# An attention and mixture-of-experts kernel on one core: instruction order taken from a list, and the last batch's attention weights turned by TensorE

## The chip, the cores and the metric

The kernel runs on one core of a Trainium2 chip. Its time is the device time of a run in microseconds (us); three runs of the kernel before gave 221.73, 222.76 and 223.56 us, with a median of 222.76. The engines are called by the profile's names: PE is TensorE (PEld its weight loads), DVE is VectorE, ACT is ScalarE, POOL is GpSimd, SP is SyncE, which here issues nearly all DMAs.

## The reference

Two steps follow each other. The first is an attention with 32 "inducing" rows, once in each direction, over four batches of 11456 tokens with 128 channels:

```python
def mab(q, kv):
    s = scale * (q @ kv.transpose(0, 2, 1))
    s = s - s.max(-1, keepdims=True)
    a = np.exp(s)
    a /= a.sum(-1, keepdims=True) + 1e-09
    return a @ kv
h = mab(I, x)                 # 32 rows per batch
attn = mab(x, h)              # every token: 32 weights times h
```

The second is a layer of 8 experts on the tokens whose skip score is positive: each such token takes the expert with the highest gate logit and adds the expert's output times its gate probability.

```python
do_compute = x @ w_skip > 0
e_idx = np.argmax(xc @ w_gate, axis=1)
y[mask] = gate_w[mask, None] * (np.maximum(xc[mask] @ w1[e], 0.0) @ w2[e])
out[do_compute] = xc + y
```

All data are float32.

## The kernel before

A batch is cut into six groups of 2048 tokens (the last has 1216; in batch 0 the small one comes first). A group is cut into four quarters q, so that a tile of a group's 32 weights per token has 4 x 32 = 128 partitions and 512 columns.

**First pass** over a group (`first`): PE forms the scores (L387), DVE their maxima (L393), ACT the exponentials (L397). PE turns them (L431) and turns x itself (L447), both into PSUM banks that ACT or DVE copy out (`copy`, L340 on ACT, L342 on DVE), and sums into the 32 rows h (L457). Five groups have their x turned by DVE from a second load instead (L424). **Between the passes** (`middle`) the rows h are normed (L540, L557), the batch's expert is chosen (L576, L577, then the DVE steps L590 to L595 and a register load on SP), its weights w1 and w2 are loaded (L719, L721; PE uses w1 at L644), and y, the expert's output for each of the 32 rows, comes out (L697, L708).

**Second pass** (`second`, `emit`): PE forms scores of 32 rows by 512 columns in each quarter (L748). DVE turns them in blocks of 32 by 32 into tile e, which has the tokens on its partitions (L753), and takes the maxima (L755); POOL or DVE subtract them (L759); ACT takes the exponentials (L762); POOL folds the halves (L768), DVE sums (L772), POOL or DVE norm (L778). DVE then turns e back into u1 (`back`, L783), with a weight's row on the partition. From u1 PE takes the gate logits. Batches 0 to 2 do it for full groups in the form called "quarters" (L840, with L844, L851, L864 behind it, and L873 to bring the gates to their place); the last batch and the small groups have 16 matmuls of 32 by 256 (L792), turned back by DVE (L801), with L803, L806, L810, L822 behind them. The weights times the gate are tile v (L882), which DVE turns into u2 (L783 again). `emit` sums hr times u1 and yr times u2 for the group into four banks (L935), copies these into two tiles `o` (L340, L342) and stores each (L945).

Tiles come from rings of fixed size: ten x tiles, eight PSUM banks, four `o`, five e and u1, two u2.

**What sets the order.** Every step is an `Op` with what it needs and the buffers it takes. `best_order` reads a rank for every step from the table PLACES, and `in_order` runs a small planner over them, with one estimated cost per step and engine. Its result is the order in which the steps are written, for each engine and for SP's DMA queue alike; where a step could run on two engines, it chose the engine. On the chip each engine works through its own list in that order and waits on semaphores.

Of the kernel before, what the change touches and what calls it, by code (L numbers as in the profile page):

```python
# [64 lines left out]
def in_order(ops, bufs):  # L65


    LAT, SLACK, RATE, LAND = 0.12, 0.1, 380.0, 1.8
    users, left = {}, {}
    for o in ops:  # L70
        left[o] = len(o.need) + len(o.behind)
        for n in o.need + o.behind:
            users.setdefault(n, []).append(o)
        for b in (*o.take, *o.free):
            b.end = b.idx = None
    free = dict.fromkeys((e for o in ops for e in o.cost), 0.0)
    wire = 0.0
    taken = {t: [] for t in bufs}
    bank = [None] * BANKS
    done = []  # L80

    def entry(o):

        at = [(e, max((d.end + (LAT if d.eng != e else 0.0) for d in o.need), default=0.0), c,
               o.spare if e == "DVE" else 0.0) for e, c in o.cost.items()]
        return o, at, sum(b.tag == "ps" for b in o.take), [b.tag for b in o.take if b.tag != "ps"]

    ready = [entry(o) for o in ops if not left[o]]
    while ready:
        up = sorted((0.0 if v is None else v.end + LAT, i) for i, v in enumerate(bank) if v is None or v.end is not None)  # L90
        c, first = [], {}
        for r in ready:
            o, at, n, tags = r
            t0 = 0.0
            if n:
                if len(up) < n:
                    continue
                t0 = up[n - 1][0]
            for tag in tags:
                k = len(taken[tag]) - bufs[tag]  # L100
                if k >= 0:
                    v = taken[tag][k].end
                    if v is None:
                        break
                    t0 = max(t0, v + LAT)
            else:
                _, t, e = min((max(t0, a, free[e]) + w + s, max(t0, a, free[e]), e) for e, a, w, s in at)
                c.append((t, e, r))
                if t < first.get(e, 1e9):
                    first[e] = t  # L110
        assert c, "a cycle of buffers"
        low = min(first.values())
        t, eng, r = min((v for v in c if v[0] <= low + SLACK and first[v[1]] == low), key=lambda v: (v[2][0].rank, v[0]))
        ready.remove(r)
        o = r[0]
        o.eng = eng
        free[eng] = o.end = t + o.cost[eng]
        if o.size:
            wire = max(wire, t) + o.size / RATE
            o.end = wire + LAND  # L120

        got = [i for v, i in up if v <= max(t, up[r[2] - 1][0])][-r[2]:] if r[2] else []
        for b in o.take:
            if b.tag == "ps":
                b.idx = got.pop()
                bank[b.idx] = b
            else:
                b.idx = len(taken[b.tag]) % bufs[b.tag]
                taken[b.tag].append(b)
        for b in o.free:  # L130
            b.end = o.end
        done.append((t, o))
        for u in users.get(o, []):
            left[u] -= 1
            if not left[u]:
                ready.append(entry(u))
    return [o for _, o in sorted(done, key=lambda v: v[0])], max(o.end for o in ops)


def best_order(ops, bufs):  # L140


    assert len(PLACES) == 3 * len(ops)
    for i, o in enumerate(ops):
        r, d, e = (DIGITS.index(c) for c in PLACES[3 * i:3 * i + 3])
        o.rank, o.spare = 64 * r + d, SPARES[e]
    return in_order(ops, bufs)[0]


DIGITS = "0123456789ABCDEFGHIJKLMNOPQRSTUVWXYZabcdefghijklmnopqrstuvwxyz-_"  # L150
SPARES = (0.0, 0.4, 1.0, 3.0, -0.5)
PLACES = (
    "Ez0Ad0DG09c0B70EU4FS0Bx3BB0HB4BM0Aq2CR09B0B50As02R08l07F07U3B209e3BJ07714n07t03b0AM12k05T02502n02A02w01H03z00u00w11U01F1"
    "1-01s42t02634602Z01f04S08O03n09C04k00v04h01_01m25u08R44W0Aj26y02I07S09l0Bg06v04R08E25-05_05P07c14D01Z17H02l33305Q00B00E0"
    "0001Q00i00420500Z10b00840r00231S00140C01C00m01A01D05y04Z05z02_04c02p41r03f41i03405v24B05B05F02Y06L03u04420I01a01z01g00S0"
    "2e00n00X23x02031p05M05727M03742x02o37X03-07o0Be0AX0Ae04z08Q03g04v02r06b03L26o01j34y02T07403W06Z47I02901q0Bf44s09A02L03F0"
    "4E06M02-02V03p4BY41h03804F26F23e07N31v2430B905809n13H08544G06938L04t03N04C09j08X03r0A008M3AD04Y0680Ci3BT17307v07a2BV07b0"
    "8A0Bp2990D117z04727e04A09805x08203Y01O09r04235k34I02O02K17x05i08F27D27p0AI0A209017A09m17g08z06P0Ao04m0500A602G04b0550Di4"
    "9h45l05d09x3Ba2Ap06j29P2AG0Av06D08i3F906V38U0A834O05X0Ai06p0D20A708N03M04K1DP09T0A10Ee1Ak3BQ0DR3Du3CM08g0Ge09G0Eq0AR09Z2"
    "6l0BU0Bu02q09Y02f03907V03o05S03E06h07m02206f44u02d23A04L01b04802703q04w01E21w02z04_09v15W07K06606Q43U05H09_04907n01o04e0"  # L160
    "8P06U09d16J0310C203P02a07f06H04N07O06d06S04V08D06141N02g3CO0DU13209303m02m03J06C09206q07y0A_27E06n12s06z07i0Bd25s05K18_0"
    "6305E07Z07Y09i09k05j18Z0DK28-0D426E03_43i0BC03y01y02W00x00L02c00g00W01X11I00a10700302434H01k00f02b00s07B00G30V01801207w0"
    "4q01T00O01P20P00c45N04p03Q44j0Ca46G02X27009S09106W09q06O0BN04r04047P1F209D0Dr43t35O01538t22v0BI06a0Gd1Ac0B_14a08h26t0670"
    "3B07l09J07Q04f05R06_1A927r03C06u37614i0DY12U3Bz0FP0G20E227-07k47W09y3710DQ09M0Ag0Da0Dp0De0830972El3BF05t0ET28r48w0Cd3AV3"
    "Cb0C80Ay0G53DF0G42FG0AT39K0Gl07h0An0Cg0BE0GF0Db0C51722B10Fb0951GM16-0D013S2Bt0GX0G60AY2DX0CS2CL0Fe39O0D_09H0880CW0GZ0BP0"
    "7C04-48926X05n09I28j3Dq08635A1D50840H80Fy3EO0DB1Gz0Fg0EJ05m0G70Gi0Fa0H20HL0Ef0Fn4Gk0Af0FZ1A51Eh0Eb2GK3Do0Cw0CQ0Bn04l0ED0"
    "E80Bv0EY0A303v0By06007_03O0Bh49t0Gm04g08p2Dt06B0Fu0Ev37d0Dj05108b0410B-05r06k03G04x08104U0EH09U06T05Y0DO0Gw0Fl08T0D709g0"
    "A-08d2AE0FI3Bl0Cz48q0E42FQ0Br0FJ0EA0D90E709b0B30EI0CY1FV0Bk09-0A409w0Aa04J08W0E505404X09V0EW05D1ER08k26R03s4EQ04Q2Ah06Y0"
    "Fw0C90Ax0CE0C30Ga48a0Cx1BX0At3CZ0Dg38o0En03D00j00l00K00o01Y00T03K00k23w02P20h01e00D10900e00A00z00601L02C00N01002j06K00-0"
    "1V01J02H25J00y4B40E_0AF3DA0Bj3D60DH45e0AA09p07q0AS08S0620DN0GB2Fm0F509o0GR1FO4FW0Ab49R36r0Cs0ES0BS0AW0E-4BD09N1450Ea0Al0"  # L170
    "Fq0Bc0F30Ds0960EB4BZ3CI0CJ0F-2FK2530EE3Cr3Cy0Cl06A0EF39Q06s16e0Bo48f0C-0Dn0FE0Dw0FD0Dk04o0DS4H91CN0C40AH0B03DL0Gb4EG1650"
# [13 lines left out]
def kernel(  # L185
# [42 lines left out]
    def bank(i):  # L228
        return banks[i]
# [979 lines left out]
```

## Time and profile before

| | |
|---|---|
| runs: median, lowest, highest | 222.76, 221.73, 223.56 us |
| profiled execution: its time, its span | 223.1, 221.4 us |
| busy PE | 195.9 us (89%) |
| busy DVE | 173.1 us (78%) |
| busy ACT | 135.6 us (61%) |
| busy POOL | 124.5 us (56%) |
| DMA, mean over the span | 257 GB/s |

The span goes from the first to the last instruction; the rest of the profiled execution's time lies around it. A busy share is an average over the whole program, so the stages have to be looked at one by one: the same page divides the span into 40 slices, and a table of windows gives the busy time of every engine between two moments. A row "after <- before: total, times, longest" in a list of waits says who waited for whom. A pair of numbers in square brackets at a row's end in a timeline is the idle time in front of the row and what ended it.

### The profile page before, as it was taken

The page shows a single profiled execution, that of the slowest core. Times are in us where ns is not written, and L with a number is a line of the kernel's source. Part 1 is how long each engine was busy: PE and PEld are TensorE (multiplying, and loading weights), DVE is VectorE, ACT ScalarE, POOL GpSimd, SP SyncE. Part 2 cuts the span into 40 slices and gives each one's busy share as a digit, 9 for nine tenths or more (in the row PEclk, how much of TensorE's full clock was granted, in tenths as well). Part 3 has the DMA queues.
Part 4 walks back from the last instruction along what each step waited for, and adds up shares of the span by engine and source line. Part 5 has one row for each costly group of instructions (what it writes and reads, how often), then busy time and mean ns, then how long its engine had stood idle before and what let it go on. Part 6 is the DMA issues. An engine that isn't in the chain of part 4 may idle for free.

```text
span 221.4 us, 6617 instructions
## 1 busy us (share of the span) xinstructions
PE 195.9 (89%) x2486; PEld 106.5 (48%) x2487; DVE 173.1 (78%) x445; ACT 135.6 (61%) x328; POOL 124.5 (56%) x306
## 2 busy tenths in 40 slices
PE   4999999979999999989999997999999897678730
PEld 1577676735665554446546352565464332232320
DVE  4355357988898998888998998698889798999840
ACT  2464574517688876864888844674977465337720
POOL 7000000546877855477589467583797996988310
PEclk9999999999999999999999999799999999999975
DMA  6999992853999985999999998921044489052990
GB/s 167 355 417 420 349 228 86 283 214 113 320 230 388 300 247 192 341 414 328 331 299 390 272 405 309 391 86 59 1 192 191 191 263 386 36 193 102 405 366 15
DMA packets 19495, 56.88 MB, mean 257 GB/s; under 512 B 2304, under 2 KB 5248, under 8 KB 19456
## 3 DMA queue, kind: packets, MB, share of 16 engines
q1 hardware_dynamic: 19168, 56.37, 74.0%
q8 instruction: 21, 0.34, 0.7%
q14 instruction: 18, 0.15, 0.2%
q10 hardware_dynamic: 288, 0.02, 0.1%
HBM read 32.92 MB, written 23.46 MB: 255 GB/s over the span
## 4 chain that ended last, share of the span: by engine, by line
PE 48%; DVE 16%; POOL 15%; DMA 9%; issue 4%; ACT 3%; SPq 1%; POOLq 0%; DVEq 0%
PE bank L447 11%; PE bank L935 9%; PE bank L387 7%; PE bank L457 7%; DMA w1s<-in_w_dram 5%; PE bank L748 5%; DMA out_dram<-o 4%; DVE u L783 4%; PE bank L431 3%; POOL e L778 3%; DVE ts L755 2%; DVE e L753 2%; POOL v L882 2%; POOL e L768 2%; POOL e L759 1%
## 5 line engine op out<-in xcount | busy, mean ns | idle before, releaser
L340 ACT COPY o<-bank 128x512 f32<-128x512 f32 (+1 forms) x90 | 45.5, 570 | 14.7 <-PE bank L935 9.2
L759 POOL TENSOR_TENSOR e<-e,ts 128x512 f32<-128x512 f32 (+1 forms) x23 | 22.8, 993 | 47.7 <-DVE cmx L590 35.6
L340 ACT COPY xt<-bank 128x512 f32<-128x512 f32 (+1 forms) x62 | 33.9, 590 | 10.0 <-PE bank L447 9.6
L447 PE MATMUL bank<-ident,x 128*128 128x128 f32 (+1 forms) x288 | 39.7, 282 | 0.0
L447 PEld LDWEIGHTS bank<-ident,x 128*128 128x128 f32 (+1 forms) x288 | 31.9, 142 | 9.2 <-issue 2.0
L387 PE MATMUL bank<-x,iT_sb 128*32 128x512 f32 (+1 forms) x192 | 25.8, 582 | 1.1 <-ACT o L340 1.1
L935 PE MATMUL bank<-u,hr 32*128 32x512 f32 (+1 forms) x192 | 25.9, 608 | 0.7 <-ACT o L340 0.7
L778 POOL TENSOR_TENSOR e<-texp,ts 128x512 f32<-128x512 f32 (+1 forms) x22 | 22.1, 1004 | 7.4 <-DVE ts L775 4.8
L457 PE MATMUL bank<-xt,a1T 128*32 128x129 f32 (+1 forms) x736 | 25.4, 276 | 0.0
L748 PE MATMUL bank<-x,hc 128*32 128x512 f32 (+1 forms) x192 | 24.9, 593 | 0.1
L935 PE MATMUL bank<-u,yr 32*128 32x512 f32 (+1 forms) x192 | 23.9, 566 | 1.2 <-DVE u L783 1.2
L882 POOL TENSOR_TENSOR v<-e,gs 128x512 f32<-128x512 f32 (+1 forms) x20 | 19.9, 1001 | 6.4 <-ACT gs L340 4.6
L457 PEld LDWEIGHTS bank<-xt,a1T 128*32 128x32 f32 (+1 forms) x736 | 18.9, 109 | 8.1 <-issue 2.2
L397 ACT ACTIVATE a<-bank,bias 128x512 f32<-128x512 f32 (+1 forms) x24 | 16.0, 666 | 10.3 <-DVE a L393 10.2
L762 ACT ACTIVATE texp<-e 128x512 f32<-128x512 f32 (+1 forms) x24 | 14.7, 613 | 7.1 <-POOL e L759 6.5
L753 DVE STREAM_TRANSPOSE e<-bank 128x512 f32<-128x512 f32 (+1 forms) x24 | 15.7, 654 | 3.0 <-PE bank L748 2.4
L783 DVE STREAM_TRANSPOSE u<-v 128x512 f32<-128x512 f32 (+1 forms) x24 | 16.1, 671 | 2.2 <-POOL v L882 1.9
L393 DVE TENSOR_SCALAR_CACHE_REDUCE a<-bank,bias 128x512 f32<-128x512 f32 (+1 forms) x20 | 14.1, 703 | 4.0 <-PE bank L387 3.6
L783 DVE STREAM_TRANSPOSE u<-e 128x512 f32<-128x512 f32 (+1 forms) x24 | 15.8, 660 | 1.1 <-POOL e L778 0.8
L755 DVE TENSOR_REDUCE ts<-e 128x16 f32<-128x512 f32 (+1 forms) x24 | 15.7, 653 | 0.8
L935 PEld LDWEIGHTS bank<-u,yr 32*128 32x128 f32 x192 | 9.3, 184 | 11.9 <-issue 5.8
L768 POOL TENSOR_TENSOR e<-texp 128x272 f32<-128x272 f32 (+1 forms) x16 | 10.5, 656 | 7.7 <-ACT texp L762 7.7
(164 smaller groups left out, 311.2 us busy)
## 6 DMA issues: line engine op xcount, KB each, us to landing
x<-in_xT_dram SPq DMA_DIRECT2D x43, 512.0 KB, 8.9
out_dram<-o SPq DMA_DIRECT2D x40, 512.0 KB, 5.3
xq<-in_xT_dram SPq DMA_DIRECT2D x20, 256.0 KB, 10.7
out_dram<-o SPq DMA_DIRECT2D x8, 304.0 KB, 4.2
w1s<-in_w_dram SPq DMA_DIRECT2D x4, 512.0 KB, 4.4
w2s<-in_w_dram SPq DMA_DIRECT2D x4, 512.0 KB, 5.4
x<-in_xT_dram SPq DMA_DIRECT2D x4, 152.0 KB, 3.0
x<-in_xT_dram SPq DMA_DIRECT2D x3, 96.0 KB, 6.9
```

Of the source, the lines that this page charges most:

```text
L340: nc.scalar.copy(out=out, in_=in_)
L387: nc.tensor.matmul(ps[q * M:(q + 1) * M, 0:W], lhsT=iT_sb, rhs=s.x[g][:, G.s1[q]:G.s1[q] + W], start=True, stop=True)
L447: nc.tensor.transpose(out=px[0:w, q * P:(q + 1) * P], in_=s.x[g][:, o:o + w], identity=ident)
L457: nc.tensor.matmul(ph[q * M:(q + 1) * M, 0:P + 1], lhsT=st["aT"][0:w, i, q * M:(q + 1) * M], rhs=xts[bx.idx][0:w, i, q, :], start=(i == 0) ...
L748: nc.tensor.matmul(ps[q * M:(q + 1) * M, 0:W], lhsT=s.hc[:, 0:M], rhs=x()[:, G.s2[q]:G.s2[q] + W], start=True, stop=True)
L753: nc.vector.transpose(out=t[:, 0:W], in_=st["ps"][:, 0:W])
L755: nc.vector.tensor_reduce(out=mx[:, 0:nb], in_=blocks(t), axis=AX.X, op=ALU.max)
L759: on(o).tensor_tensor(out=blocks(t), in0=blocks(t), in1=wide(st["mx"]), op=ALU.subtract)
L778: on(o).tensor_tensor(out=blocks(st["e"]), in0=ev(M), in1=wide(st["i"]), op=ALU.mult)
L783: nc.vector.transpose(out=st[f"u{k}"][:, 0:W], in_=st[src][:, 0:W])
L882: on(o).tensor_tensor(out=blocks(u), in0=blocks(st["e"]), in1=wide(st["gm"]), op=ALU.mult)
L935: nc.tensor.matmul(bank(bp[q].idx)[:, 0:G.w1], lhsT=m[r, :], rhs=st[k][r, c], start=(k == "u1"), stop=(k == "u2"))
```

## The change

First, the planner is gone. `in_order` now reads a list ORDER, which names the next step, the engine it runs on, and the number of every buffer it takes. All steps stand in that list, so the order of all engines, the engine of each step that can run on two, and the PSUM banks are new in every stage.

Second, the five full groups of the last batch (TURNED) are computed in another way. e and v are no longer turned back by DVE; PE turns each in four transposes of 128 by 128 into a bank, and ACT or DVE copy it into u1 or u2. In this form four neighbouring blocks of 32 tokens share the partitions where the four quarters did. Their logits come from four matmuls of 128 by 32 that leave the tokens on the partitions, so nothing has to be turned behind them; the gate takes the form of the quarters without its L859, L868, L873 and the copy behind it. The four banks of `emit` are copied into the group's own x tile, in runs of 32 columns, and the stores go from there, two for each group as before.

```diff
-def in_order(ops, bufs):
...
-def best_order(ops, bufs):
...
-PLACES = (
-    "Ez0Ad0DG09c0B70EU4FS0Bx3BB0HB4BM0Aq2CR09B0B50As02R08l07F07U3B209e3BJ07714n07t03b0AM12k05T02502n02A02w01H03z00u00w11U01F1"
...
+def in_order(ops):
+
+    digits = iter(DIGITS.index(c) for c in ORDER)
+    order = []
+    for d in digits:
+        o = ops[64 * d + next(digits)]
+        assert o.eng is None
+        o.eng = ENGINES[next(digits)]
+        assert o.eng in o.cost
         for b in o.take:
+            b.idx = next(digits)
+        order.append(o)
+    assert len(order) == len(ops)
+    return order
+
+
+ORDER = (
+    "00000E010U020k0301170041600-04022061505203308140730A1300930I1510B30K140J30C130L20F1510D20M131E050G20O140N30V1600P30H30Y1"
...
+    TURNED = ((), (), (), (0, 1, 2, 3, 4))
...
-            G.quarters = G.nb == MAXB and b < B - 1
+            G.turned = G.g in TURNED[b]
+            assert not G.turned or G.cols == GC and b == B - 1
+            G.quarters = G.nb == MAXB and (b < B - 1 or G.turned)
...
+        def turn(o, buf, src):
+            for i in range(Q):
+                nc.tensor.transpose(out=bank(buf.idx)[:, i * P:(i + 1) * P], in_=st[src][:, i * P:(i + 1) * P], identity=ident)
+
+        def turned(o, buf, k):
+            if k == 2:
+                st["u2"] = wk.tile([P, GC // Q], F32, tag="u2", bufs=BUFS["u2"], name=f"u2_{b}_{g}")
+            copy(o, st[f"u{k}"], bank(buf.idx))
+
+        def logits_t(o):
+            pl = st["pl"] = bank(bl.idx)
+            st["lt"] = wk.tile([P, MAXB // 2 * M], F32, tag="lt", bufs=BUFS["lt"], name=f"lt_{b}_{g}")
+            for i in range(Q):
+                nc.tensor.matmul(pl[:, i * M:(i + 1) * M], lhsT=st["u1"][:, i * P:(i + 1) * P],
+                                 rhs=s.lrq.rearrange("p q k -> p (q k)"), start=True, stop=True)
+
+        def logits_in(o):
+            copy(o, st["lt"][:, 0:P], st["pl"][:, 0:P])
+
+        def most(o):
+            st["gx"] = gxs[:, b, g, :]
+            nc.vector.tensor_reduce(out=st["gx"], in_=qv()[:, :, 0:E - 1], axis=AX.X, op=ALU.max)
...
+        if keep and G.turned:
+            b1, b2 = Buf("ps"), Buf("ps")
+            o = L.add({"PE": 0.66}, lambda o: turn(o, b1, "e"), o_v, take=[b1])
+            st["o1"] = o = L.add({**act(W), **dve(W)}, lambda o: turned(o, b1, 1), o, free=[b1])
+            o = L.add({"PE": 0.6}, logits_t, o, s.o_lrq, take=[bl, blt])
...
+            o = L.add({"PE": 0.66}, lambda o: turn(o, b2, "v2"), o, take=[b2], free=[bv])
+            st["o2"] = L.add({**act(W), **dve(W)}, lambda o: turned(o, b2, 2), o, take=[st["b2"]], free=[b2])
+            return st, L
...
+        def spread(o, j):
+            v = s.x[g].rearrange("c (q i j r) -> c i q j r", q=Q, i=Q, j=Q)[:, :, :, j, :]
+            copy(o, v, bank(bp[j].idx).rearrange("c (i q r) -> c i q r", i=Q, q=Q))
...
+        if G.turned:
+            c = [L.add({**act(G.w1), **dve(G.w1)}, lambda o, j=j: spread(o, j), m, free=[bp[j]]) for j in range(Q)]
+            for h in range(2):
+                L.add({"SP": 0.08}, lambda o, h=h: store_x(o, h), *c, free=[s.xbuf[g]] if h == 1 else [], size=G.cols * 0.256)
+            return
```

Three places show how the order moves. In the names the numbers behind a tile are its batch and group and a running number; the line numbers of the changed kernel are its own.

SP's DMA queue where batch 0 loads its expert's weights (x_1_4 is group 4 of batch 1), before:

```order
L358 DMA x_1_3_463<-in_xT_dram 128x1024 x2
L358 DMA x_1_4_600<-in_xT_dram 128x1024 x2
L601 TENSOR_LOAD ei_0_621
L601 ISA x2
L719 ISA
L719 DMA w1s_0_644<-in_w1_dram 128x1024
L721 ISA
L721 DMA w2s_0_646<-in_w2_dram 128x1024
```

and now:

```order
L300 DMA x_1_3_415<-in_xT_dram 128x1024 x2
L543 TENSOR_LOAD ei_0_624
L543 ISA x2
L661 ISA
L661 DMA w1s_0_654<-in_w1_dram 128x1024
L663 ISA
L663 DMA w2s_0_656<-in_w2_dram 128x1024
L300 DMA x_1_4_688<-in_xT_dram 128x1024 x2
```

The two loads of x_1_4 stood in front of the weights and now stand behind them.

DVE where batch 2 chooses its expert (cmx to ei; SP waits for ei), before:

```order
L783 STREAM_TRANSPOSE u1_1_5_1731<-e2_1_5_1730 128x320
L753 STREAM_TRANSPOSE e2_2_0_2007<-bank5_75 128x512
L755 TENSOR_REDUCE ts0_2_145<-e2_2_0_2007 128x16
L590 TENSOR_REDUCE cmx_2_2049<-pl_2_2038 128x1
L591 SCALAR_TENSOR_TENSOR cnts_2_2048<-pl_2_2038,cmx_2_2049,codes_96 128x8
L593 TENSOR_REDUCE code_2_2052<-cnts_2_2048 128x1
L595 TENSOR_SCALAR ei_2_2054<-code_2_2052 128x1
```

and now:

```order
L725 STREAM_TRANSPOSE u2_1_4_2027<-v2_1_4_2005 128x512
L725 STREAM_TRANSPOSE u2_1_3_2035<-v2_1_3_2017 128x512
L532 TENSOR_REDUCE cmx_2_2049<-pl_2_2046 128x1
L533 SCALAR_TENSOR_TENSOR cnts_2_2048<-pl_2_2046,cmx_2_2049,codes_96 128x8
L535 TENSOR_REDUCE code_2_2052<-cnts_2_2048 128x1
L537 TENSOR_SCALAR ei_2_2054<-code_2_2052 128x1
```

The first turned scores of batch 2 (e2_2_0) stood in front of the choice; now two steps of batch 1 do, and e2_2_0 comes later. On SP's queue the loads of x_3_4 also moved from in front of these weights to behind them.

PE in the second pass of the last batch, before:

```order
L792 MATMUL bank1_71<-u1_3_1_2753,lr_3_179 32x256 x8
L792 MATMUL bank3_73<-u1_3_4_2893,lr_3_179 32x256 x8
L748 MATMUL bank2_72<-x_3_5_2161,hc_3_2697 32x320 x4
L792 MATMUL bank3_73<-u1_3_3_2876,lr_3_179 32x256 x8
L935 MATMUL bank2_72<-u1_3_2_2812,hr_3_2668 128x512
```

and now, at the same stage:

```order
L780 MATMUL bank1_71<-ident_83,e2_3_2_2799 128x128 x4
L690 MATMUL bank6_76<-x_3_5_2153,hc_3_2695 32x320 x4
L780 MATMUL bank7_77<-ident_83,e2_3_3_2854 128x128 x4
L791 MATMUL bank2_72<-lrq_3_180,u1_3_2_2800 128x32 x4
L780 MATMUL bank3_73<-ident_83,v2_3_1_2989 128x128 x4
L791 MATMUL bank2_72<-lrq_3_180,u1_3_3_2855 128x32 x4
L780 MATMUL bank6_76<-ident_83,e2_3_4_2902 128x128 x4
L918 MATMUL bank3_73<-u1_3_1_2786,hr_3_2675 128x512
```

Where PE had the logits of 32 by 256 and then sums, it now has turns (L780) and the new logits (L791) of several groups interleaved, and other groups' sums (L918) after them.

## Rows read from the trace of the kernel before

**Rows 1.** Windows by stage: start:end, length, busy by engine, PE clock, DMA.
```profile
core 0: us, PE busy (x) PEld busy (x) DVE busy (x) ACT busy (x) POOL busy (x), PEclk, DMA share, GB/s
0.00:11.13 11.13, 7.94 (x39) 4.04 (x41) 4.12 (x7) 3.74 (x8) 4.12 (x41) 1.00 0.79 261
11.13:35.30 24.17, 24.10 (x342) 16.75 (x341) 12.12 (x28) 14.34 (x30) 0.00 (x0) 1.00 1.01 340
35.30:78.20 42.90, 41.37 (x571) 24.98 (x570) 37.99 (x100) 27.84 (x70) 27.06 (x55) 1.00 0.79 244
78.20:123.80 45.60, 44.36 (x597) 23.68 (x597) 40.80 (x102) 34.71 (x87) 29.53 (x64) 1.00 0.94 315
123.80:168.03 44.23, 42.30 (x577) 22.75 (x573) 38.15 (x105) 29.66 (x75) 29.08 (x60) 0.96 0.56 209
168.03:213.16 45.13, 35.31 (x368) 13.86 (x369) 39.34 (x105) 25.27 (x60) 34.68 (x87) 1.00 0.62 238
213.16:221.40 8.24, 0.57 (x2) 0.48 (x2) 0.57 (x3) 0.00 (x0) 0.00 (x0) 0.50 0.33 115
```

**Rows 2.** Waits from 168 to 214 us: total, times, longest.
```profile
PEld bank L935 <- DVE u L783: 5.7, 9, 1.8
PE bank L792 <- DVE u L783: 3.8, 4, 1.6
PEld bank L935 <- ACT o L340: 3.5, 5, 0.8
```

**Rows 3.** Timeline of PE in batches 0, 1 and 2: start, length.
```profile
46.57 0.64 PE L644 MATMUL bank<-w1s,hc 128*32 128x256 f32 x8 [1.17 <-DMA w1s<-in_w_dram]
...
98.13 1.06 PE L387 MATMUL bank<-x,iT_sb 128*32 128x512 f32 x8 [1.05 <-ACT o L340]
...
137.95 1.04 PE L644 MATMUL bank<-w1s,hc 128*32 128x256 f32 x8 [1.18 <-DMA w1s<-in_w_dram]
```

**Rows 4.** Windows around the weights of batch 2, columns as in Rows 1.
```profile
135.00:138.00 3.00, 1.37 (x28) 0.42 (x24) 2.82 (x9) 1.82 (x4) 1.61 (x5) 1.00 0.93 341
138.00:141.30 3.30, 3.30 (x19) 1.33 (x20) 1.16 (x3) 2.20 (x7) 1.84 (x5) 0.51 1.02 411
```

**Rows 5.** Timeline of SP's DMA issues around the weights of batches 0 and 2.
```profile
24.54 14.80 SPq L358 DMA_DIRECT2D x<-in_xT_dram  x4
41.58 0.35 SPq L719 DMA_DIRECT2D w1s<-in_w_dram  x1
...
127.71 1.20 SPq L358 DMA_DIRECT2D x<-in_xT_dram  x2
131.21 0.34 SPq L719 DMA_DIRECT2D w1s<-in_w_dram  x1
```

**Rows 6.** Line L719, the four loads of w1, from issue on.
```profile
DMA to landing us min/median/max: 3.6/4.4/6.6
```

**Rows 7.** Timeline of PE: single steps.
```profile
127.33 0.39 PE L576 MATMUL bank<-ws_sb,hc 128*128 128x8 f32 x2
127.57 0.37 PE L577 MATMUL bank<-ws_sb,hc 128*128 128x9 f32 x2
...
162.21 1.47 PE L447 MATMUL bank<-ident,x 128*128 128x128 f32 x12
...
193.75 1.97 PE L792 MATMUL bank<-u,lr 32*32 32x256 f32 x32 [0.67 <-DVE u L783]
```

**Rows 8.** Groups by form: count, busy us, mean ns, idle before.
```profile
L340 ACT COPY o<-bank 128x512 f32<-128x512 f32 x77 | 40.7, 595 | 12.4 <-PE bank L935 6.9 <-PE bank L792 2.2 <-ACT o L340 1.2
L762 ACT ACTIVATE texp<-e 128x512 f32<-128x512 f32 x20 | 12.8, 640 | 6.5 <-POOL e L759 6.0 <-DVE e L759 0.5
L783 DVE STREAM_TRANSPOSE u<-v 128x512 f32<-128x512 f32 x20 | 14.1, 704 | 1.0 <-POOL v L882 0.7
L801 DVE STREAM_TRANSPOSE lt<-bank 128x256 f32<-128x256 f32 x5 | 2.1, 410 | 0.0
L342 DVE COPY o<-bank 128x512 f32<-128x512 f32 x3 | 2.0, 680 | 0.0
```

More of the change, by code (lines that the diff above doesn't have):

```diff
@@ L62, in __init__ @@
         self.tag, self.end, self.idx = tag, None, None
-def in_order(ops, bufs):
[L68 to L122, printed above, removed]
-        for b in o.take:
[L124 to L137, printed above, removed]
@@ new lines @@
+ENGINES = ("SP", "PE", "DVE", "ACT", "POOL")
+DIGITS = "0123456789ABCDEFGHIJKLMNOPQRSTUVWXYZabcdefghijklmnopqrstuvwxyz-_"
+def in_order(ops):
[6 more added lines that the diff above has]
+        assert o.eng in o.cost
+        for b in o.take:
+            b.idx = next(digits)
+        order.append(o)
+    assert len(order) == len(ops)
+    return order
@@ L882, in scale2 @@
             on(o).tensor_tensor(out=blocks(u), in0=blocks(st["e"]), in1=wide(st["gm"]), op=ALU.mult)
-        o = L.add(pe(W), scores, s.o_hc, last["s2"], take=[bs, be, st["b1"]], free=[s.xbuf[g]] if keep else [])
+        o = L.add(pe(W), scores, s.o_hc, last["s2"], take=[bs, be, st["b1"]], free=[s.xbuf[g]] if keep and not G.turned else [])
         last["s2"] = o if keep else None
@@ L892, in second @@
         o_v = L.add({**pool(W), **dve(W)}, norm, o, free=[bex])
+        if keep and G.turned:
[3 more added lines that the diff above has]
+            o = L.add({"PE": 0.6}, logits_t, o, s.o_lrq, take=[bl, blt])
+            o = L.add({**act(P), **dve(P)}, logits_in, o, free=[bl])
+            o_m = L.add({"DVE": 0.27}, most, o)
+            o_x = L.add({"ACT": 0.6}, gexp_q, o)
+            o_c = L.add({"POOL": 0.75}, claim_q, o_m)
+            s.o_claim.append(o_c)
+            o = L.add({"DVE": 0.54}, gate_q, o_x)
+            o = L.add({"POOL": 0.22}, pick, o, o_c)
+            o = L.add({**pool(W), **dve(W)}, scale2, o, take=[bv], free=[be, blt])
+            o = L.add({"PE": 0.66}, lambda o: turn(o, b2, "v2"), o, take=[b2], free=[bv])
+            st["o2"] = L.add({**act(W), **dve(W)}, lambda o: turned(o, b2, 2), o, take=[st["b2"]], free=[b2])
+            return st, L
         st["o1"] = o = L.add(dve(W), lambda o: back(1, "e"), o_v)
@@ L1165 @@
     with tc.manual_schedule():
-        for o in best_order(all_steps(), BUFS):
+        for o in in_order(all_steps()):
             o.fn(o)
```

72 lines of the change are left out of this document (38 added, 34 removed).

## The prediction

> **What bounds the kernel now.** I read the page's engine shares first, then the busy times by stage, then the waits inside the stage that looks different, then the timeline at the few places where PE stands still.
>
> The shares alone (PE 89%, DVE 78%) say "PE-bound, with a little slack". The stages say something else [rows 1]. I cut the span at the steps L540, which close a batch's first pass. From 11.1 to 168.0 us PE is busy for 152.1 of 156.9 us: there it is the bound and nothing that other engines save can shorten it. In the last stage, from the last L540 at 168.03 to the final step L1020 at 213.16, PE is busy for 35.3 of 45.1 us and idle for 9.8, while DVE works 39.3 and POOL 34.7. That is the second pass of the last batch with no first pass left to fill PE. What PE waits for there is DVE's turning back of e and v into u: 5.7 us in front of the sums and 3.8 in front of the logits; another 3.5 is ACT copying banks out [rows 2]. The 8.2 us behind L1020 hold two small DVE steps and the last stores, and the change leaves them as they are.
>
> Before that stage PE loses time in small pieces. Three have a cause that the order of the list decides [rows 3]: 1.17 us at 46.6 and 1.18 at 138.0, both waiting for the expert's w1, and 1.05 at 98.1, waiting for a bank that ACT had to empty. The wait at 138 costs more than itself: PE was busy for only 1.37 of the 3 us before, and from 138.0 to 141.3 its granted clock is 0.51, the lower of its two levels, 1.2 GHz [rows 4]. PE was busy all that time, so about half of the 3.3 us, 1.6, was lost.
>
> **The change, part by part.** Times are worked out in the profiled execution's span of 221.4 us; its own time is 223.1, so 1.7 lie around the span, and it is 0.3 above the median of the runs.
>
> *PE's new work.* Five groups are turned twice, four transposes each: 40. Twelve transposes in a row took 1.47 us, 0.12 each [rows 7], so 4.9 us. Five times the logits of 32 by 256 go away; two groups of them took 1.97 us, 0.98 each [rows 7]. In their place stand four matmuls with a full 128 by 128 weight and 32 columns, and a float32 matmul shows as two rows. No row is quite that; nearest is L576 and L577, 8 or 9 columns on a 128 by 128 weight: the second pair starts 0.24 us after the first (0.12 a pass) and takes 0.37 to its end (0.19 a pass). Eight passes are therefore 1.0 to 1.5 us. The passes of a group follow each other without a wait, so I take 1.2, near the spacing: 0.2 more than before, 1.1 for five groups. Sum: PE 6.0 us more (5.0 to 7.5), all of it in the last stage, on the engine that is the bound elsewhere: 41.3 us of work there.
>
> *DVE* loses ten turns at 0.70 and five turns of logits at 0.41 [rows 8], 9.1 us. It gets back eight copies out of banks at 0.68 (two of u, six into x), 5.4 us, and some subtractions and norms that the list moved over from POOL. Its last stage goes from 39 to 36 to 38 us. *ACT* takes the other eight copies of u at 0.595, 4.8 us, four copies of logits and a second exponential per group: 25 becomes about 33. Its copies into x write runs of 32 columns. The plain copy costs 0.595 and an exponential that writes runs of 32 costs 0.640 [rows 8], so fourteen of them cost at most 0.6 us more, off the path. *POOL* loses the subtraction of the logits and two small steps per group and goes from 35 to about 30. So in the last stage PE becomes the longest list at 41.3, DVE follows at 36 to 38, and the others have room.
>
> *The last stage.* It cannot be shorter than 41.3. I went through the new lists by hand, giving each step the duration of its row, and found PE standing at four places. First, between L540 and the scores of group 0: den, hr, its transpose and hc follow each other, and PE has only three small steps to fill in; about 1 us. Second, in front of w2's matmuls, which wait for gsel: DVE turns the scores of group 3 ahead of it; 0.5. Third, in front of the logits of group 2, whose u1 DVE copies only after two row sums; 0.4. Last, in front of the small group's second sums: DVE copies a bank of group 4 before it scales and turns v of group 5; about 1. That is 2.8, and the stage takes 44.1 instead of 45.1: 1.0 less. The ends are no idle time at all (41.3) and the present 9.8 (51.1); I stay near the lower one because in the earlier stages, where PE had other groups' work between as it has here, it stood still for 0.1 to 1.9 us in 24 to 46 [rows 1]. A turn by PE puts a copy between PE and the next PE step, where before DVE's result was used directly, but the list puts other groups' work in that gap (the interleaved rows of PE), and that is the cover. Without it each of the ten turns shows up as a copy of 0.6.
>
> *The stages before.* The loads of x_1_4 now stand behind batch 0's weights. Before, their issue ended at 39.3 and the weights were issued at 41.6 [rows 5], so 1 MB was in flight in front. PE could start L644 5.0 us after the issue [rows 3]; the fastest of the four w1 landed in 3.6 [rows 6], and 1.2 us earlier is all that is needed. In batch 2 the weights were issued 3.6 us after L577 started [rows 5, 7], since DVE first turned a tile of scores and took its maxima; they took 6.6 us to land [rows 6] behind the loads of x_3_4. Now neither stands in front. I count both waits and the low clock as gone: 1.2 + 1.2 + 1.6 = 4.0 us. The price is that x_1_4, x_3_4 and others are issued later; PE takes them up over ten microseconds of its work after that, so I cost it at nothing. If that cover failed, a load at the landing times seen here, up to 6.6, would be waited for. The stores, moved on SP's queue in many places, hold loads behind them until ACT has copied. The bank wait of 1.05 may go or come back elsewhere, since all bank numbers are new. I put 1.0 for new waits of that size, between nothing and the 4.0 gained. So 3.0 less.
>
> *Stores.* A group's two stores now wait for all four copies, up to two copies later than the first did. The last ones are those of the small group, in `o` tiles, as before; costed at nothing.
>
> **Sum.** 221.4 - 3.0 - 1.0 = 217.4 us of span, 219.1 of time, and 218.8 against the median.
>
> One rule of the Trainium skill speaks against the change. What the row shows first: from 11.1 to 35.3 us PE does the first passes of batch 0, a good part of it transposes, and its clock stays at 1.00, full speed, 2.4 GHz [rows 1]. The Trainium skill, page "TensorE: Matmul & The Clock Gate", Part 4 (PE-mode transpose), says that transposes don't count as PE activity for the clock the way matmuls do. Going by that, the last stage, with 40 of them among pauses, could fall to the lower level, which is the fourth rival below; the row gives it little.
>
> **Rivals.**
>
> *No net change.* The new list moves waits about in front and saves none, and only the last stage's 1.0 remains: 221.8. For it: PE is already busy for 97% of that stretch, and each of the three waits is only about 1 us. Against: two of them have a named cause that the order removes.
>
> *Slower: the round trip is not covered.* Place: the ten turns in the last stage. u1 and u2 wait in ACT's list behind copies of finished groups, and PE, which takes its list in order, stands in front of the logits or sums that need them. Then the idle 9.8 us stay while PE has 6.0 more: with the 3.0 gained in front, 222.8 + 3.0 = 225.8. It decides from 6.8 us of idle PE between L540 and L1020 on. For it: ACT gets 8 us more. Against: ACT still has 11 of 44 us free and DVE's wait, the larger one, goes.
>
> *More than forecast.* The bank wait goes too, no new wait comes, and the last stage leaves PE 1.5 idle: 5.0 + 2.3 = 7.3 less, 215.5. For it: from 11 to 35 us PE shows 0.3% idle, so a list without waits is possible. Against: a chain of dependent steps at the very end leaves PE idle whatever the order.
>
> *Slower: the clock.* After 1.6 us of idle PE in 3 the clock fell before [rows 4]; the last stage's waits could do the same. PE at 1.2 GHz there costs 1.6 us per 3.3 us, and 12 if it lasts for the 25 us in which turns are made: 220.4 to 231.
>
> That the change does not do what it says can be left out: the turns and stores stand in the lists.
>
> **Numbers.** About 1% (2.2 us) is what a measurement of this kernel tells from no change, so faster means below 220.5 and slower above 225. Forecast (216.5 to 220.5): 0.50. More: 0.16. No net change, with its neighbours from 220.5 to 225: 0.20. Round trip: 0.10. Clock: 0.04. Faster 0.66, same 0.20, slower 0.14. The range goes from 213.5, 2 below the rival that gains most, to 225.0, which takes in PE's upper bound of 7.5; outside lie some 0.04 below and 0.12 above. The forecast's own range is 216.5 to 220.5.
>
> **What would show it.** L644 without a wait for w1 in batches 0 and 2, and a clock of 1.00 between them. From the last L540 to L1020 about 44 us, PE busy for 41 of them, DVE's waits of 5.7 and 3.8 gone. Transposes at 0.12 and logits at 1.0 to 1.5 per group. ACT's copies into x at 0.6. The prediction is wrong if PE's idle in the last stage exceeds 7, if new waits of more than 3 us stand in the first 168 us, or if the clock falls between the turns.

## The result and the profile after

The changed kernel takes 216.8 us (median of 4 runs, 215.1 to 218.4) against 222.6 for the kernel before: 5.8 us less, ratio 0.971, 95% interval 0.966 to 0.976. One of the four, 218.4, is a slow run; the ratios here and below leave slow runs out, while the times are medians of all. The profiled execution took 217.5 with a span of 215.7. Forecast were 218.8, with a range of 213.5 to 225.0, and "faster" as the likeliest. The sum came out 2 us too high, and both of its terms were off, in opposite directions.

The stages of the changed kernel, cut at its own four L482 (before: L540) and at L1016 (before: L1020). Columns as in [rows 1]:

```profile
0.00:11.13 11.13, 7.07 (x38) 4.52 (x43) 4.36 (x6) 3.98 (x9) 4.02 (x41) 1.00 0.83 281
11.13:36.41 25.28, 25.06 (x345) 17.08 (x342) 9.56 (x24) 16.19 (x36) 0.00 (x0) 1.00 0.93 318
36.41:75.44 39.03, 38.94 (x558) 23.23 (x557) 34.09 (x94) 28.51 (x70) 25.52 (x51) 1.00 0.86 263
75.44:121.12 45.68, 44.98 (x619) 24.69 (x617) 42.65 (x111) 34.65 (x89) 31.96 (x71) 1.00 0.93 321
121.12:162.05 40.93, 39.19 (x569) 21.61 (x565) 37.33 (x104) 30.04 (x79) 30.29 (x66) 1.00 0.63 217
162.05:207.13 45.08, 41.70 (x369) 22.03 (x369) 36.17 (x91) 28.21 (x70) 31.18 (x72) 0.92 0.59 228
207.13:215.70 8.57, 0.40 (x6) 0.30 (x2) 0.71 (x3) 1.04 (x3) 0.00 (x0) 0.51 0.50 185
```

Read against [rows 1]: the last L482 comes at 162.05, where L540 came at 168.03, 6.0 earlier. The last stage, in which TensorE now turns the five full groups, is as long as before (45.08 and 45.13), and its clock column fell from 1.00 to 0.92. By this profile the whole gain is the front's.

In front, the three waits of [rows 3] are gone. The timeline of PE shows w1's matmuls of batches 0 and 2 without the bracket that named the DMA, and the clock between them stays up (windows; before it was 0.51 in [rows 4]):

```profile
45.91 0.40 PE L586 MATMUL bank<-w1s,hc 128*32 128x256 f32 x4
132.89 0.64 PE L586 MATMUL bank<-w1s,hc 128*32 128x256 f32 x8
```

```profile
133.00:136.30 3.30, 3.17 (x37) 2.21 (x40) 2.86 (x10) 3.27 (x8) 2.38 (x5) 1.00 1.03 391
```

In the last stage DVE's waits of [rows 2] are gone too. What PE waits for instead (waits, last stage: total, times, longest), and the place of the first (timeline of ACT, then of PE):

```profile
ACT o L282 <- DMA out_dram<-o: 2.7, 2, 2.6
PE bank L918 <- ACT x L282: 1.6, 1, 1.6
PE bank L690 <- ACT o L282: 0.9, 1, 0.9
```

```profile
177.70 1.07 ACT L282 COPY o<-bank 128x512 f32<-128x512 f32 x2 [2.57 <-DMA out_dram<-o]
```

```profile
178.34 0.64 PE L690 MATMUL bank<-x,hc 128*32 128x512 f32 x4 [0.95 <-ACT o L282]
```

This is a chain of three. ACT waits 2.57 us for a store, since an `o` tile is free only when its sums are written out; until then it can't copy the next bank, and PE waits 0.95 us for a bank that ACT has still to copy. The stores of the third batch come together there: the DMA does next to nothing from 166 to 171 us and is full from 173 to 183 (windows, the two last columns are its share and GB/s):

```profile
166.00:171.00 5.00, 5.00 (x48) 2.18 (x44) 4.21 (x13) 2.10 (x6) 3.68 (x12) 0.96 0.01 4
173.00:183.00 10.00, 8.72 (x66) 4.54 (x66) 8.02 (x19) 5.77 (x14) 5.79 (x13) 0.85 0.99 383
```

The clock fell twice in the last stage. Four windows of that trace, each fall with the three microseconds ahead of it:

```profile
160.00:163.00 3.00, 2.37 (x53) 1.38 (x41) 2.86 (x14) 2.50 (x9) 2.39 (x7) 1.00 0.25 101
163.00:166.20 3.20, 2.84 (x30) 1.02 (x25) 3.13 (x7) 0.67 (x4) 2.95 (x6) 0.50 0.59 234
177.00:180.00 3.00, 1.88 (x18) 0.70 (x17) 1.27 (x4) 2.10 (x6) 1.44 (x4) 1.00 1.02 412
180.00:183.30 3.30, 3.30 (x25) 1.89 (x25) 3.13 (x8) 2.05 (x6) 2.41 (x6) 0.51 0.96 390
```

PE worked 6.1 us at the lower of its two levels, 1.2 GHz, so up to half of that, 3.1 us, was lost.

The new steps themselves (groups by form in the last stage):

```profile
L282 ACT COPY x<-bank 128x512 f32<-128x512 f32 x14 | 7.4, 594 | 3.1 <-PE bank L918 2.2 <-PE bank L972 0.7
L284 DVE COPY x<-bank 128x512 f32<-128x512 f32 x6 | 3.9, 677 | 1.2 <-PE bank L918 1.1
```

Copies into x in runs of 32 columns cost what plain ones cost in [rows 8] (595 and 680 ns).

### The profile page after: what moved, and what is told of

Its sections match the earlier page's. It is cut to its first block, busy times and chain, and to the rows that moved or that the text cites. A ratio compares the mean times of both kernels' runs of the same rounds, so it can differ in the third digit from the quotient of the medians.

```text
span 215.7 us, 6608 instructions
## 1 busy us (share of the span) xinstructions
PE 197.3 (91%) x2486; PEld 113.5 (53%) x2487; DVE 164.9 (76%) x430; ACT 142.6 (66%) x351; POOL 123.0 (57%) x299
## 4 chain that ended last, share of the span: by engine, by line
PE 78%; DVE 7%; ACT 6%; DMA 3%; issue 1%; POOL 0%; SPq 0%; ACTq 0%; POOLq 0%
PE bank L918 18%; PE bank L389 15%; PE bank L329 9%; PE bank L399 9%; PE bank L690 8%; PE bank L373 4%; DMA out_dram<-o 3%; PE bank L780 3%; ACT o L282 2%; PE bank L805 2%; PE bank L791 2%; PE bank L734 2%; DVE sel L188 1%; ACT xt L282 1%; PE bank L639 1%
## 5 line engine op out<-in xcount | busy, mean ns | idle before, releaser
L282 ACT COPY o<-bank 128x512 f32<-128x512 f32 (+1 forms) x73 | 36.9, 561 | 16.8 <-PE bank L918 13.5
L282 ACT COPY xt<-bank 128x512 f32<-128x512 f32 (+1 forms) x66 | 36.5, 591 | 14.9 <-PE bank L389 14.6
L918 PE MATMUL bank<-u,hr 32*128 32x512 f32 (+1 forms) x192 | 26.3, 618 | 1.8 <-ACT x L282 1.6
L701 POOL TENSOR_TENSOR e<-e,ts 128x512 f32<-128x512 f32 (+1 forms) x21 | 21.0, 1001 | 7.7 <-DVE ts L697 5.9
L690 PE MATMUL bank<-x,hc 128*32 128x512 f32 (+1 forms) x192 | 24.0, 590 | 0.9 <-ACT o L282 0.9
L918 PE MATMUL bank<-u,yr 32*128 32x512 f32 (+1 forms) x192 | 24.0, 571 | 0.0
L849 POOL TENSOR_TENSOR v<-e,gs 128x512 f32<-128x512 f32 (+1 forms) x21 | 21.4, 1023 | 4.1 <-ACT gs L282 3.5
L720 POOL TENSOR_TENSOR e<-texp,ts 128x512 f32<-128x512 f32 (+1 forms) x20 | 20.4, 1023 | 4.2 <-DVE ts L717 2.8
L561 POOL TENSOR_TENSOR lr<-pl,lm 128x16 f32<-128x16 f32 x4 | 0.8, 212 | 37.6 <-DVE lm L555 36.8
L710 POOL TENSOR_TENSOR e<-texp 128x272 f32<-128x272 f32 (+1 forms) x17 | 11.3, 667 | 7.9 <-ACT texp L704 7.9
L918 PEld LDWEIGHTS bank<-u,yr 32*128 32x128 f32 x192 | 10.2, 191 | 9.5 <-issue 7.8
L725 DVE STREAM_TRANSPOSE u<-v 128x512 f32<-128x512 f32 (+1 forms) x19 | 12.2, 649 | 0.2
```

The costliest lines, as they stand in the source:

```text
L282: nc.scalar.copy(out=out, in_=in_)
L690: nc.tensor.matmul(ps[q * M:(q + 1) * M, 0:W], lhsT=s.hc[:, 0:M], rhs=x()[:, G.s2[q]:G.s2[q] + W], start=True, stop=True)
L701: on(o).tensor_tensor(out=blocks(t), in0=blocks(t), in1=wide(st["mx"]), op=ALU.subtract)
L720: on(o).tensor_tensor(out=blocks(st["e"]), in0=ev(M), in1=wide(st["i"]), op=ALU.mult)
L849: on(o).tensor_tensor(out=blocks(u), in0=blocks(st["e"]), in1=wide(st["gm"]), op=ALU.mult)
L918: nc.tensor.matmul(bank(bp[q].idx)[:, 0:G.w1], lhsT=m[r, :], rhs=st[k][r, c], start=(k == "u1"), stop=(k == "u2"))
```

## Experiments

Times are medians; a ratio is to the kernel before, run on the same chip beside it (its medians there: 222.0, 223.3 and 222.7 us). To compare stages across kernels I use two lengths of each profile: A, up to the last batch's L482, and B, from there to the end. (In the kernels whose edit adds lines, L482 and L1016 are L483 and L1023; I keep the numbers of the changed kernel.) The kernel before has A 168.0 and B 53.4, the changed one 162.1 and 53.7.

**1. The halves apart: front_only and turn_only.** The two lists differ by four steps when cut at some 148 us, and were joined there.

```diff
-    TURNED = ((), (), (), (0, 1, 2, 3, 4))
+    TURNED = ((), (), (), ())                # front_only; turn_only keeps it
 ORDER: up to the cut the changed list, behind it the rest in the order of before
        # turn_only: up to the cut the order of before, behind it the changed list
```

> The steps of the kernel before (nothing is turned by TensorE), with the changed list's order up to some 148 us, in the third batch's second half, and the order of before from there on. Theory 1: the gain of 5.8 us is all the front's, because the last stage (from the last batch's L482 to L1016) took 45.1 us in both kernels. Then this takes 217 (216.3 to 218) and its last stage 45 us at a clock of 1.00. Rival, by the prediction's own sum: the front is worth 3.0 and the turning the rest: then 219.6 (219 to 220.5).

> The other half: the order of before up to some 148 us, with its waits for the weights, and from there the changed list with the five groups turned by TensorE and stored from their x tiles. Theory 1: 222 (221.3 to 223), with a last stage of 45 us in which the clock falls once or twice. Rival, by the prediction's sum: the turning saves 1 to 3: 219.5 to 221.5.

front_only: 219.0, ratio 0.984 (0.977 to 0.991), A 163.6, B 54.1. turn_only: 223.6, ratio 1.006 (1.002 to 1.010), A 167.4, B 52.9. The front alone saves 4.4 us of A and the turning alone no time: Theory 1 holds for who gains, but front_only is 2 us slower than it said, at the edge of the rival's 219 to 220.5: its B is 0.7 longer than before, with 3.3 us at low clock in it, and the seam added waits of 1.16 and 0.45. turn_only's stage from L482 to L1016 took 44.1, the very number forecast, though 7 us of it ran at low clock. The halves don't add up to the whole: 1.6% less and 0.6% more make 1.0% less, against 2.9% for both together. Seam and clock take part of the difference; the rest these two runs leave open.

**2. Is it the transposes that let the clock fall? plain_turn.**

```diff
-                nc.tensor.transpose(out=bank(buf.idx)[:, i * P:(i + 1) * P], in_=st[src][:, i * P:(i + 1) * P], identity=ident)
+                nc.tensor.matmul(bank(buf.idx)[:, i * P:(i + 1) * P], lhsT=st[src][:, i * P:(i + 1) * P], rhs=ident, start=True, stop=True)
```

> The changed kernel with its 40 turns written as plain matmuls against the identity in place of transposes; nothing else moves. A plain 128x128 matmul took about 0.21 us a piece in this trace (L650, L482) against 0.165 for a turn, so 40 cost 1.8 more. Theory a: the clock falls at 163 and 180 us because transposes do not keep it up: it stays at 1.00 from 175 on, which gives back about 1.5: 216.5 to 217.5. Theory b: the falls follow the waits of PE (0.95 us at 178.3 for ACT) and stay: 218 to 219, clock 0.5 over some 3 us near 181.

224.7 us, ratio 1.011 (1.004 to 1.017): 8 slower than the changed kernel. Timeline of PE in plain_turn, and the same step in the changed kernel:

```profile
190.46 1.16 PE L780 MATMUL bank<-ident,e 128*128 128x128 f32 x8
191.54 0.74 PE L690 MATMUL bank<-x,hc 128*32 128x320 f32 x8
```

```profile
188.40 0.66 PE L780 MATMUL bank<-ident,e 128*128 128x128 f32 x4
188.98 0.75 PE L690 MATMUL bank<-x,hc 128*32 128x320 f32 x8
```

From the start of a turn to the next step it is 1.08 and 0.58: a transpose of 128 by 128 shows as one row, a float32 matmul as two. Ten turns cost 5 us more, where I had expected 1.8. The stage is 5.7 us longer; another 2.4 stand behind L1016 (10.9 us to the end, against 8.6), which no run explains. And a fall stayed (windows of plain_turn):

```profile
161.47:212.26 50.79, 45.98 (x408) 27.56 (x409) 36.42 (x91) 28.78 (x70) 30.86 (x72) 0.93 0.52 203
178.00:185.00 7.00, 5.87 (x38) 3.32 (x31) 3.38 (x9) 3.11 (x8) 3.78 (x9) 0.51 0.62 249
```

Theory b is nearer, though the time misses both: no transposes of v or e are left, and the clock still fell for 7 us, behind a wait of 1.04. The fall at 163 is missing, but falls come and go between executions of one program (section 8), so that one profile each says only that the clock can fall without these transposes. The prediction weighed a rule of the Trainium skill (page "TensorE: Matmul & The Clock Gate", Part 4, PE-mode transpose), by which transposes don't count as PE activity the way matmuls do; this run does not show it at work.

**3. The o tiles: own_tiles, and once more as own_again.** The third batch's groups 2 to 4 leave through their own x tiles, which no later load takes.

```diff
+            G.own = b == B - 2 and G.g in (2, 3, 4)
 def stream(o, q):
+            if G.own:
+                copy(o, s.x[g][:, G.s1[q]:G.s1[q] + G.w1], bank(bp[q].idx)[:, 0:G.w1])
+                return
 def store(o, h):
+            if G.own:
+                nc.sync.dma_start(out=out[:, t0:t0 + 2 * G.w1], in_=s.x[g][:, G.s1[2 * h]:G.s1[2 * h] + 2 * G.w1])
+                return
```

> The changed kernel, with the sums of groups 2, 3 and 4 of the third batch copied into their own x tiles too (no later load takes these) and stored from there, so that the four o tiles stop being waited for. Theory: ACT's 2.6 us wait for a store (L282 o, 177.7) goes, PE's 0.95 at L690 with it, and the clock's fall at 180 to 183 with that: 1.0 + 1.6 less, 214.2 (213.5 to 215). Rival: only the wait goes and the clock falls all the same: 215.8. Second rival: the end hangs on the stores, whose DMA is full from 202 to 211 us, and nothing is gained: 216.5 to 217.

> own_tiles once more, beside tail2 and with more rounds: 212.5 to 215. Its first profile had lost 3.7 us to a low clock at 84 to 88 us, where the same instructions had run at full clock in the changed kernel; now that fall should be elsewhere or missing, and the last stage again 41 to 42 us where no fall lies in it.

215.1 (ratio 0.958, 0.950 to 0.966) and 214.9 (0.965, 0.959 to 0.971): some 1% below the changed kernel. ACT's wait for a store and PE's 0.95 are gone in both, as the theory has it (215.1 lies just outside its 213.5 to 215). B is 50.0 and 50.9, against 53.7. Windows of own_tiles: its last stage, in which no fall lies, and the fall that it had elsewhere instead:

```profile
166.41:207.79 41.38, 38.68 (x368) 20.97 (x368) 35.88 (x91) 28.39 (x70) 30.96 (x72) 1.00 0.64 249
84.00:87.80 3.80, 3.80 (x59) 3.76 (x60) 1.66 (x5) 1.32 (x6) 2.26 (x8) 0.56 0.84 257
```

At full clock the turned stage takes 41.4 us, with 38.7 of work for PE. In own_again the fall at 84 is missing, and one stands at 164 to 168: that the clock's fall goes with the wait is not shown. (The profile of own_tiles is its longest execution, 218.2 us. The expectation of own_again puts 3.7 us of that down to the fall. The same steps took some 1.5 longer there than in own_again; the rest are two waits of PE, 1.04 at 34.6 and 1.19 at 133.7.)

**4. The same without turning: front_own.** front_only with the edit of own_tiles.

> The kernel of front_only (changed order to 148 us, VectorE turns, last stage as before), with groups 2 to 4 of the third batch stored through their x tiles as in own_tiles. It took 219.0 without. Theory: there the last stage waits for u of VectorE (3.2 + 0.9 us) and not for the o tiles, so nothing is won: 218.5 to 219.5. Rival: the o tiles hold up every last stage, and it is 216 to 217 without any turning by TensorE.

216.7, ratio 0.972 (0.962 to 0.983), A 162.7, B 52.0. Theory fails, and the time is the rival's. ACT's waits for stores in the last stage, in front_only and then here:

```profile
ACT o L282 <- DMA out_dram<-o: 4.2, 3, 2.5
ACT o L283 <- DMA out_dram<-o: 1.7, 2, 1.5
```

With that went a wait of PE for ACT of 1.25. The fall of front_only at 187 is missing too, but it is not shown to hang on this: the wait just ahead of it, 1.56 for DVE's u, is here as well, and nothing falls. The rival's "every last stage" is too much, since in the kernel before ACT waits for no store there. With three groups stored elsewhere, a kernel in which TensorE turns nothing is as fast as the changed one (0.972 and 0.971). Its last stage (window), at full clock as well:

```profile
162.69:206.88 44.19, 35.06 (x369) 13.91 (x369) 39.16 (x105) 25.65 (x60) 34.66 (x87) 1.00 0.64 243
```

Beside own_tiles this is what turning does when the o tiles are out of the way and no fall lies in the stage: PE 3.6 us more work, DVE 3.3 less, the stage 2.8 shorter, B 2.0 shorter.

**5. The turned stage behind the old front: turn_own.** turn_only with the edit of own_tiles.

> turn_only (the order of before up to 148 us, turned last stage) with the third batch's groups 2 to 4 stored from their x tiles. If the o tiles are what the turned stage waits for, and the front counts apart from it: 3 less than turn_only beside the same before, 219.5 to 221, and no clock fall that follows a wait for a store. Rival: without the front's new order the turned stage is as long as before, 222 to 223.5.

221.7, ratio 0.996 (0.991 to 1.000); A 170.5, B 50.3. Its stage from L482 to L1016 (window):

```profile
170.46:211.83 41.37, 38.69 (x369) 20.97 (x369) 35.87 (x91) 28.38 (x70) 30.86 (x72) 1.00 0.63 250
```

That is own_tiles' stage to a hundredth, so at full clock its length does not depend on the front. The o tiles were not what held up turn_only, though: ACT waited for no store there either, and what its stage lost was 7 us at low clock, which no run ties to them. The total misses the 219.5 to 221 by a little; in the profile A, with its waits for w1 (1.5 and 1.3) and a fall at 139, is 2.5 longer than in the kernel before. With the o tiles out of the way the halves nearly add up: 2.8% (front_own) and 0.4% (here), against 3.5 and 4.2% for own_tiles.

**6. The prediction's cause for the front, the loads alone: w_first.** Two steps of before's list move. DVE's earlier choice of the expert, which the prediction also named for batch 2, stays as before.

```diff
 SP, first batch                    SP, third batch
-load x_1_4                        -load x_3_4
 weights (w1s, w2s)                 weights (w1s, w2s)
+load x_1_4                        +load x_3_4
```

> The kernel before, its order kept in every place but two: the load of x for group 4 of the second and of the fourth batch is issued behind the weights of the first and the third batch, not ahead of them. Theory: the two waits of TensorE for w1s (1.2 and 1.2) go and the low clock behind the second (1.6) with them: 218.0 to 219.5. Rival 1, what the prediction put against it: the later x is waited for and a part comes back, 219.5 to 221. Rival 2: the waits pass to the next late thing and nothing is won, 221.5 to 222.5.

224.1, ratio 1.002 (0.995 to 1.008): nothing. In the first batch 0.47 of the 1.17 stay. In the third the wait for w1 does go, and its 1.18 come back as more a little later (timelines of PE, then of ACT):

```profile
46.90 0.64 PE L586 MATMUL bank<-w1s,hc 128*32 128x256 f32 x8 [0.47 <-DMA w1s<-in_w_dram]
136.93 0.61 PE L586 MATMUL bank<-w1s,hc 128*32 128x256 f32 x8
143.63 0.55 PE L389 MATMUL bank<-ident,x 128*128 128x128 f32 x3 [2.21 <-ACT o L282]
```

```profile
143.16 0.73 ACT L282 COPY o<-bank 128x304 f32<-128x304 f32 x2 [2.70 <-DMA out_dram<-o]
```

It is the o tiles again: PE is a microsecond earlier, x's loads now stand between the weights and the stores, and ACT wants an o tile before its store is out. In that stage of the changed kernel ACT waits for no store. Behind the wait the clock falls, from 144.6 to 148. Rival 2 is right that nothing is won, and the two loads alone explain none of the gain. The profile is of one of the longer of ten runs (225.4 us; they go from 220.9 to 226.3): that the wait for the store stands in all of them is not shown.

**7. The end: tail and tail2.** own_tiles with the small group's last steps ahead of other work. (The names below are those of steps in the kernel; pick takes the small group's gates, scale2 and back make its weighted u2, sums_of its sums.)

```diff
 POOL, last steps                   DVE, last steps
+pick (small group)                +low's copy (tail2)
 theirs                            +scale2, back of v (small group)
-pick (small group)                 x copy of group 4
                                   -low's copy, -scale2, -back of v
-sums_of of the small group: banks 3, 7, 1, 5
+sums_of of the small group: banks 2, 4, 6, 1
```

> own_tiles with three moves at its end: the small group's gates and second weights go ahead of the counting on POOL and of the last x copy on DVE, and its sums take four banks that are free. That takes away TensorE's 1.6 us wait for ACT's x copies before the last sums, and L1016 comes some 0.8 to 1 us earlier. Theory 1: the end hangs on the stores (DMA full from 202 to 211 us in the changed kernel), so the time is that of own_tiles, 212.4 to 215. Theory 2: the end hangs on TensorE's last sums, and 0.8 to 1 us is gained: 211.5 to 213.

> tail once more, with its slip mended: there the last sums still waited 1.34 us, for a bank that DVE freed only behind an x copy. Here the marking's copy, the small group's second weights and their transpose go ahead of that x copy, so that the last sums wait for nothing but u: from the last batch's L482 to L1016 40 to 40.8 us in place of 41.4 and 42.0. Theory 1: the end hangs on the stores, which keep the DMA full for the last 9 to 10 us before it: L1016 comes 1 us earlier, the DMA falls silent when it did before, and the time stays that of own_again within 0.5. Theory 2: the end follows L1016 by 8.4 to 8.6 us as in all the turned kernels so far, and the time is 0.8 to 1.4 less than own_again's.

tail: 214.4 (0.964, 0.951 to 0.977), with a wait of 1.34 for a bank in the place of the one for ACT, so it decides nothing. tail2: 213.9 (0.962, 0.957 to 0.967), from L482 to L1016 40.95. Windows of tail2, the stage and what is behind it:

```profile
163.87:204.82 40.95, 39.27 (x368) 21.10 (x369) 36.04 (x92) 28.66 (x71) 30.76 (x72) 1.00 0.64 247
204.82:209.50 4.68, 0.36 (x2) 0.27 (x2) 0.67 (x3) 0.76 (x3) 0.00 (x0) 0.79 0.95 357
209.50:213.80 4.30, 0.00 (x0) 0.00 (x0) 0.00 (x0) 0.00 (x0) 0.00 (x0) 0.50 0.07 20
```

L1016 comes 0.43 us sooner after L482 than in own_tiles, and B is 49.9 in place of 50.0: what was won went into the end, as Theory 1 has it. That is weak, since the end is not as fixed as the expectation says: from L1016 on it took 8.61 us in own_tiles and 8.98 in tail2, but also 8.97 in turn_own, whose end is that of own_tiles. The medians of tail2 and own_again differ by 0.9 us, which is Theory 2's number; but as ratios, 0.962 and 0.965, their intervals overlap, so neither theory is shown. own_tiles and tail2 are faster than the kernel before; against the changed one (0.966 to 0.976) they gain some 1%, and the intervals touch.

**8. The changed kernel again: after_again.**

> The changed kernel once more, beside the others: 216 to 218. If the clock's falls at 163 and 180 us belong to its order, they stand in the same places; if they come by chance of an execution, one of them at least is elsewhere or missing.

218.1 (4 runs, 215.8 to 220.7), A 162.6, B 52.5. One fall, not two, and it is twice as long (window):

```profile
164.90:171.60 6.70, 6.70 (x36) 3.00 (x36) 5.38 (x16) 0.43 (x3) 5.58 (x17) 0.50 0.07 27
```

At 178 to 181 us its clock is 1.00 and the wait of 0.95 is missing; probably what ran slower behind 165 gave the stores time. So the same program falls in partly different places, and a fall costs, estimated as half of its 3.2 to 6.7 us, 1.6 to 3.4.

## Why the prediction was right, and where it was not

**What bounds it: right.** PE is the bound in front and waits in the last stage; both trace and experiments bear that out.

**The front, 3.0 less: too small, and its cause incomplete.** Measured are 6.0. The terms that I counted came: the waits for w1 (1.2 and 1.2) and the low clock (1.6). The bank wait at 98, left open, went too (1.05), and the 1.0 for new waits came in small pieces: PE's other waits between the first L482 and the last grew from 0.7 us to 1.9, none above 0.45. The first L482 itself comes 1.1 later. Windows from the first to the last, before and now:

```profile
35.30:168.03 132.73, 128.03 (x1739) 71.41 (x1737) 116.95 (x305) 92.21 (x231) 85.67 (x179) 0.99 0.77 257
36.41:162.05 125.64, 123.11 (x1739) 69.53 (x1737) 114.06 (x307) 93.20 (x237) 87.78 (x187) 1.00 0.81 269
```

Of the 7.1 us between them only 2.2 are idle time of PE; 4.9 are busy time, for as many matmuls. The low clock is 1.6 of that. The other 3.3 were in none of my terms, and I can't place them by a row. The step that failed is "The loads of x_1_4 now stand behind batch 0's weights", with the later loads costed "at nothing": done alone, that move and the one of x_3_4 are worth nothing (w_first), and in its profile the third batch's gain comes back as a wait for an o tile whose store is late. The sentence that stores hold loads behind them saw the queue, but not who waits for the tile. That the whole list is worth 4 to 6 us is shown by A: with the new list in front it is 161.5 to 163.9 in eight profiles (166.4 in own_tiles, with its fall and waits), with the old one 167.4 to 170.5 in four. Which of its other moves do it was not taken apart; DVE's earlier choice was moved in no run alone.

**PE's new work, 6.0: too large.** At full clock PE has 3.4 us more than before in own_tiles, and 3.6 more than in front_own. Steps moved over the cut at L482 hardly count: 16 matmuls of the small group's logits came into the stage (0.8), and 16 other small ones left it (0.7). A turn mostly takes 0.5 to 0.6 us to the next step, 0.12 to 0.15 a transpose, a little more than [rows 7] gave, and a group's logits 0.9, 0.3 less than I took; by spacing some 5 us more in all. The rest of the difference I can't place by a row. A likely part, not shown, is that a step behind a wait counts its whole length as busy, and before there were more of those. The 41.7 in the changed kernel's profile looks like the 41.3 of my sum by luck: some 3 of it is low clock.

**The last stage, 1.0 less: the idle sum nearly right, its places wrong, and the clock left out.** Idle is 3.4 against 2.8 (the four places add up to 2.9). Only the first (0.36 and small pieces) and the last (1.61) are there, and the last stands in front of the small group's first sums and waits for ACT's copies of x, not for DVE. The o tiles, which cost 0.95, were not on the list. Then the clock: it fell for some 6 us in the profile, on my own terms a sign that the prediction was wrong. I gave that rival 4%. Its price, 1.6 for 3.3 us, was near; its chance was not. I let one row speak against it, the 1.00 of batch 0's first passes [rows 1]; but there PE is busy for 24.10 of 24.17 us, which says little about a stage with pauses. In seven of the eleven profiles with the new front or the new stage a fall lay between 130 us and L1016. Had none come, own_tiles says what the stage would have been: 41.4 and the 0.95 that its missing wait saves, so an estimate of 42.3, and the rival "more than forecast" would have been nearer.

**The sum: right by two errors.** The gain was put 3.0 too low in front, 0.9 too high in the stage, and 0.3 too high behind L1016 (8.57 us, before 8.24). That these partly cancel is luck. The time, 216.8, lies between forecast (218.8) and that rival (215.5). "Round trip not covered" stayed away: PE waits for no copy of u.

What stays open: where and when the clock falls. It follows stretches in which PE waits or does small steps (2.37 and 1.88 of 3 us above), but the kernel before had PE busy for only 0.49 of the 2 us from 188 to 190 and did not fall. One pattern stands in the profiles: in four of the nine with the turned stage (the changed kernel twice, turn_only, own_again) a fall begins 1 to 2.5 us behind the last L482, where the new list leaves PE small steps; in the four with the old stage none does. No run changes those steps, so the cause stays open.

## What to carry to other kernels

When a wait is moved out of the way, ask which buffer the earlier engine will run into next: here it was twice the same four output tiles, and in the last stage tiles of finished inputs took their place. Judge a stage's work at full clock, from an execution in which nothing fell, and give a fall a price and a real chance wherever waits and small steps break up PE's work. A gain that comes from a rewritten list is worth splitting at a place where both lists have done the same steps; the cause one names may be worth nothing by itself.

## What the runs showed of the hardware

A 32 by 128 copy on DVE took 1.95 us in the kernel before and 2.88 in the changed one, both while POOL was filling constants (busy for 2.92 of the 3 us from 1.5 to 4.5 in the changed kernel); DVE's 128 by 128 copy out of a bank, just behind it, took 0.29. Timeline of DVE in the changed kernel:

```profile
1.53 2.88 DVE L188 COPY sel<-ident 32x128 f32<-32x128 f32 x1 [1.41 <-POOL ident masks.py:199]
5.29 0.29 DVE L192 COPY rep<-bank 128x128 f32<-128x128 f32 x1 [0.88 <-PE bank L190]
```

It cost little here: PE's first scores end at 7.20 us, and at 6.99 before. Why the copy takes so long is not shown: the lines up to it are the same in both kernels, POOL's fills among them, and yet it took 1.95 and 2.88, and no run makes this copy without the fills.
